# Two-stage MoE after thresholded attention on one core: grouped row blocks, a second place for half of the split weights, a new order

## The chip, the cores and the metric

One NeuronCore of a Trainium2 chip runs the whole program. The metric is device microseconds, from launch to end of one execution; of several executions the median counts.

## The reference, cut to what matters

```python
scores = 1/sqrt(64) * q @ k.T                       # 4 batches x 8 heads, 576 rows, width 64
thresh = max(scores, -1) - tau
scores = where(scores >= thresh, scores, -1e9) - max(...)
attn   = exp(scores); attn = attn / (sum(attn, -1) + 1e-9)
x      = (attn @ v) as 2304 tokens x 512
h = x @ w_in;  g = 0 if h <= -1, h if h >= 1, else (h + 1)**2 / 4;  x = g @ w_out     # first MLP, d_ff 2048
h = x @ w_in2; g = h - tanh(h);                                     out = g @ w_out2  # second MLP
```

The weights come as float64, everything else as float32.

## The kernel before, in words

The matrix products of the MLPs keep float32 accuracy by splitting each operand into a high and a low part (`hi`, `lo`, both float32r) and adding three products: hi x hi, lo x hi, hi x lo.

**MLPs.** The 2304 tokens are five token blocks: the first 512 rows of each of the four batches (blocks 0 to 3) and the four leftovers of 64 rows (block 4, 256 wide). Each MLP has 16 chunks of d_ff, 128 wide, so a block is 2 x 16 = 32 steps, 160 in all; step j has block T, MLP M, chunk s. A step multiplies the block with a chunk of `w_in` into a PSUM bank `ph` (`m_h`), applies the gate (`m_act` on ACT, `m_dve` on DVE), splits the result (`m_split`: copy `gh`, then subtraction `gl`, mostly on POOL) and adds the product with a chunk of `w_out` to four banks `s` (`m_out`).

**Weights.** In block 0 a chunk is loaded raw (`w_load`, two halves into `w64`), decoded from float64 to float32 (`w_dec`: `top` on ACT, then `wr` on DVE) and split (`w_split`: `wi`/`wo`, copy on ACT, subtraction mostly on POOL) into two pairs of hi and lo, one for `w_in` (`wi`), one for `w_out` (`wo`), each 512 KB in a ring of three. `w_store` writes both pairs to DRAM (`wf0i`, `wf0o`, `wf1i`, `wf1o`); blocks 1 to 4 read them back (`w_get`).

**Attention.** The unit is a row block: 128 rows of one head against its 576 keys. `u_qk` on PE writes scores `s`; `u_max` on DVE takes the negated row maximum; `u_exp` on ACT; `u_mask` on DVE applies the threshold, sums the row and turns the sum into a factor `rs` (tensor_scalar, reciprocal, each on one column). Then `u_hi` (ACT) and `u_lo` (POOL) split the weights into two f16 parts `a`, and `u_tr` transposes them by DMA into `at`. Batches 0 and 1 are "narrow" (`NARROW`): per row block, `u_dot` runs 14 products of width 64 into a bank `ph`, and `u_put` on DVE scales the 64 columns into `xw`. Of batch 0's four head pairs the last is `direct`: PE transposes, and there is no f16 split. `v_load`, `v_max`, `v_sc1`, `v_sc2`, `v_split` load and split the values. Batches 2 and 3 are "wide" (`pv`). Batch 0's attention runs ahead of step 0 (below: the prologue), batch 1's beside block 0, batch 2's beside block 1, batch 3's beside block 2, and batch 0's leftover rows beside block 3.

**What sets the order.** `kernel` gives every call a place on a scale of steps (`when`, `at`, L953 on), less a number from the table `PRE` by function and stage. `Program.issue` (L261) then plays the engines forward with assumed durations and lets each take the ready instruction with the lowest number. What comes out is a fixed order for each engine: PE, DVE (VectorE), ACT (ScalarE), POOL (GpSimd) and SP, which issues all DMAs. On the chip each works its order from front to back. The PSUM banks are two `ph` and six in three tiles `s`; `ph` serves gates, products with values and small transposes in turn.

The lines that the steps below touch: `u_mask` L603, `u_tr` L642, `u_dot` L658, `u_put` L677, `v_load` L696, `w_get` L826, `w_dec` L832, `w_store` L846, `w_split` L852. Almost every instruction is recorded by `rec` and so shows as L354 in the profile.

Of the kernel before, what the change touches and what calls it, by code (L numbers as in the profile page):

```python
# [21 lines left out]
D = 64  # L22
# [66 lines left out]
    "load_k": (7.27, -15.44, 8.94, 0.00),  # L89
    "load_q": (3.73, 6.44, 24.95, 0.00),  # L90
    "m_act": (0.00, -5.32, -0.24, -7.95),
    "m_dve": (0.00, 11.52, -21.89, -14.88),
    "m_evac": (0.00, -4.26, 4.07, -23.40),
    "m_h": (0.00, -1.15, -0.74, 2.14),
    "m_out": (0.00, -3.74, -0.36, 2.07),
    "m_split": (0.00, -1.26, 7.97, 1.61),
    "prep_k": (-15.59, 0.87, 7.96, 0.00),
    "prep_q": (21.35, 4.08, -22.11, 0.00),
    "pv": (0.00, 0.00, 2.86, 0.00),
    "u_dot": (-4.92, -3.40, 0.00, 0.00),  # L100
    "u_exp": (23.08, 16.66, 42.89, 0.00),
    "u_hi": (10.52, 34.89, 8.23, 0.00),
    "u_lo": (-15.45, 16.69, 11.25, 0.00),
    "u_mask": (1.51, -2.24, 3.82, 0.00),
    "u_max": (10.16, -1.25, -4.45, 0.00),
    "u_put": (19.81, -1.30, 0.00, 0.00),
    "u_qk": (-1.85, 25.10, 3.18, 0.00),
    "u_tr": (5.19, -3.00, 19.56, 0.00),
    "v_load": (1.71, -6.79, 1.05, 0.00),
    "v_max": (5.82, -0.49, -4.93, 0.00),  # L110
    "v_sc1": (-2.99, 15.36, 1.20, 0.00),
    "v_sc2": (-2.52, -2.20, 18.08, 0.00),
# [16 lines left out]
W_LO = "PVPPPPPVPPVPPPPP"  # L129
UNIT = (0.0, 0.05, 0.1, 0.2, 0.3, 0.4, 0.5)  # L130
# [32 lines left out]
class Program:  # L163
# [169 lines left out]
def attention_moe_moe2(ctx: ExitStack, tc: tile.TileContext, qd, kd, vd, tau, w1, w2, ident, out):  # L333
# [61 lines left out]
    def dve(name, **kw):  # L395
# [26 lines left out]
    def dma(out, in_):  # L422
# [17 lines left out]
    wf = [[dram.tile([NF, 128, 1024], F32, name=f"wf{m}{p}") for p in "io"] for m in range(2)]  # L440
    wr = const("wr", [128, 3, 1024])
# [29 lines left out]
    )  # L471
    m4_r = ring("m4", 2, [4, 1])
# [7 lines left out]
    for b, mains, tail in plan:  # L480
        for hp in range(H // 2):
# [85 lines left out]
    def transpose(out, in_):  # L567
        rec("SP", 1290, nc.sync.dma_start_transpose, serve=1100 * in_.shape[0] * width(in_) / (128 * 1152), out=out, in_=in_)
# [89 lines left out]
    def u_dot(i):  # L658
# [4 lines left out]
        if t.direct:  # L663
            for c in range(5):
                n = 128 if c < 4 else 64
                mm(u.p[:, 0:D], u.et[0:n, 128 * c:128 * c + 128], v.raw[0:n, 2 * (t.hp % 2) + e, c], c == 0, c == 4)
            return
        for x in range(2) if e is None else (e,):
            h = 2 * (t.hp % 2) + x
            o = u.p[:, 64 * x:64 * x + 64] if e is None else u.p[:, 0:64]  # L670
            for c in range(5):
                mm(o, u.at[:, c], v.t[:, h, c, x, :], c == 0, False)
                mm(o, u.at[:, c], v.t[:, h, c, 1 - x, :], False, False)
            for c in range(4):
                mm(o, u.at[:, 5 + c], v.t[:, h, c, x, :], False, c == 3)

    def u_put(i):  # L677
        t, e, m = units[i]
        u = U.pop(i)
        if e is None:  # L680
            t.xt = xt_r()
        elif t.xf is None:
            t.xf = xf_r()
        for x in range(2) if e is None else (e,):
            o = t.xt[:, 64 * x:64 * x + 64] if e is None else t.xf[:, 128 * m + D * e:128 * m + D * e + D]
            src = u.p[:, 64 * x:64 * x + 64] if e is None else u.p[:, 0:64]
            if t.direct:
# [417 lines left out]
```

## Time and profile before

| what | us |
|---|---|
| three runs | 1081.36, 1089.78, 1090.70 |
| median | 1089.78 |
| profiled execution, span from first to last instruction | 1082.6 |
| profiled execution, time of its own | not listed beside its span |
| TensorE busy | 1030.0 |
| ScalarE, VectorE, GpSimd busy | 632.4, 629.2, 504.0 |

How to read it: busy times of different engines overlap, so they don't add up to the span. The engine with the largest share is the one to ask first, but what a change is worth in a stage is decided by the wait that ends last in that stage. The profile counts from the first instruction of the program.

### The profile page before, as it was taken

Reading aid. Unit: us, or ns where it says so; the run is one execution under the profiler, and the core shown is the slowest. Engines: PE = TensorE matmul, PEld = TensorE weight load, DVE = VectorE, ACT = ScalarE, POOL = GpSimd, SP = SyncE. Lnnn points to the kernel's source line nnn. Section 1 sums busy time; section 2 is a strip of 40 time slices with the busy share of each in tenths; the row PEclk is TensorE's granted clock in tenths of the full one; section 3 lists DMA queues with packets and bytes.
Section 4 is the critical chain, followed back from the end, with each engine's and each line's share of the span. In section 5 each row is a group of like instructions: output and inputs, shape, how many; then the busy total and the mean of one; then the engine's idle time right before and its main releaser. Section 6 shows DMA issues by size and latency. Waiting matters only on the chain.

```text
span 1082.6 us, 17257 instructions
## 1 busy us (share of the span) xinstructions
PE 1030.0 (95%) x5826; PEld 831.0 (77%) x5826; DVE 629.2 (58%) x1380; ACT 632.4 (58%) x1158; POOL 504.0 (47%) x510
## 2 busy tenths in 40 slices
PE   5789999999999999999999999999999999998997
PEld 3567777767777788778888888778877878888986
DVE  5987978898898766674347665742253331113432
ACT  5778777768776777676457777764353332222332
POOL 3654778768686555445345555444333212220000
PEclk8999999999999999999999999999999999999999
DMA  6999999999999998889679988897586655557997
GB/s 148 176 229 335 313 319 320 297 275 353 352 336 314 315 243 231 226 227 232 209 206 277 266 212 217 211 230 207 171 269 194 178 189 183 188 193 285 369 343 248
DMA packets 231384, 272.93 MB, mean 252 GB/s; under 512 B 170240, under 2 KB 170368, under 8 KB 231296
## 3 DMA queue, kind: packets, MB, share of 16 engines
q1 hardware_dynamic: 231296, 271.83, 86.5%
q8 instruction: 46, 0.75, 0.3%
q14 instruction: 42, 0.34, 0.1%
HBM read 193.40 MB, written 38.27 MB: 214 GB/s over the span
## 4 chain that ended last, share of the span: by engine, by line
PE 70%; DVE 12%; ACT 8%; DMA 5%; issue 4%; POOL 1%; SPq 0%; ACTq 0%; DVEq 0%; POOLq 0%
PE ph L354 35%; PE s L354 35%; DVE small L354 3%; DMA w<-in_w_dram 2%; ACT e L354 2%; DVE wr L354 2%; DVE e L354 2%; DMA vr<-in_vd_dram 2%; DVE g L354 1%; DVE xw L354 1%; ACT a L354 1%; DVE ph L354 1%; DMA wo<-wf0o 1%; ACT top L354 1%; DMA at<-w 1%
## 5 line engine op out<-in xcount | busy, mean ns | idle before, releaser
L354 PE MATMUL ph<-xh,wi 128*128 128x512 f32 x1024 | 271.1, 399 | 4.0 <-DVE g L354 3.7
L354 POOL TENSOR_TENSOR a<-e,a 128x512 f16<-128x512 f32 x236 | 180.9, 785 | 188.9 <-ACT a L354 172.4
L354 POOL TENSOR_TENSOR gl<-g,gh 128x512 fp32r<-128x512 f32 x114 | 152.3, 1336 | 199.1 <-ACT gh L354 179.4
L354 PEld LDWEIGHTS ph<-xh,wi 128*128 128x128 f32 x1024 | 188.0, 189 | 45.4 <-DVE g L354 6.2
L354 PE MATMUL s<-gh,wo 128*128 128x512 f32 (+1 forms) x640 | 157.4, 377 | 5.2 <-ACT gh L354 1.9
L354 PE MATMUL s<-wo,gh 128*128 128x512 f32 x576 | 155.1, 398 | 1.1 <-ACT w L354 0.7
L354 PE MATMUL ph<-xl,wi 128*128 128x512 f32 x512 | 144.8, 396 | 0.2 <-DVE xl L354 0.2
L354 DVE SCALAR_TENSOR_TENSOR e<-s,small,e 128x576 f32<-128x576 f32 x129 | 104.8, 813 | 67.1 <-ACT small L354 66.4
L354 DVE TENSOR_REDUCE small<-s 128x1 f32<-128x576 f32 x144 | 108.2, 752 | 47.7 <-PE s L354 46.8
L354 ACT ACTIVATE gh<-g 128x512 fp32r<-128x512 f32 (+1 forms) x152 | 88.2, 581 | 78.5 <-DVE g L354 76.2
L354 DVE TENSOR_TENSOR g<-ph,t 128x512 f32<-128x512 f32 (+1 forms) x80 | 50.8, 635 | 142.2 <-ACT t L354 138.9
L354 PEld LDWEIGHTS s<-gh,wo 128*128 128x128 f32 x640 | 112.0, 191 | 26.4 <-ACT gh L354 4.2
L354 PEld LDWEIGHTS s<-wo,gh 128*128 128x128 f32 x576 | 105.2, 188 | 22.9 <-ACT gh L354 1.1
L354 ACT ACTIVATE e<-s,small 128x576 f32<-128x576 f32 x129 | 94.9, 736 | 44.6 <-DVE small L354 41.7
L354 ACT ACTIVATE t<-ph 128x512 f32<-128x512 f32 (+1 forms) x80 | 44.1, 552 | 120.6 <-PE ph L354 120.4
L354 PEld LDWEIGHTS ph<-xl,wi 128*128 128x128 f32 x512 | 95.9, 188 | 23.2 <-DVE xl L354 1.2
L354 PE MATMUL s<-gl,wo 128*128 128x512 f32 (+1 forms) x320 | 89.4, 381 | 4.5 <-ACT xh L354 2.1
L354 DVE TENSOR_TENSOR ph<-ph,t 128x512 f32<-128x512 f32 (+1 forms) x80 | 51.4, 643 | 70.1 <-ACT t L354 69.2
L354 ACT ACTIVATE t<-ph,small 128x512 f32<-128x512 f32 (+1 forms) x80 | 51.4, 642 | 66.4 <-PE ph L354 66.2
L354 ACT ACTIVATE a<-e 128x576 f16<-128x576 f32 x118 | 80.1, 679 | 6.8 <-DVE e L354 4.8
L354 PE MATMUL s<-wo,gl 128*128 128x512 f32 x288 | 82.3, 393 | 1.0 <-ACT w L354 1.0
L354 PEld LDWEIGHTS s<-gl,wo 128*128 128x128 f32 x320 | 57.6, 190 | 15.8 <-ACT xh L354 3.4
(107 smaller groups left out, 1513.6 us busy)
## 6 DMA issues: line engine op xcount, KB each, us to landing
w<-in_w_dram SPq DMA_DIRECT2D x64, 512.0 KB, 6.0
wi<-wf0i SPq DMA_DIRECT2D x64, 512.0 KB, 4.1
wo<-wf0o SPq DMA_DIRECT2D x64, 512.0 KB, 4.3
wi<-wf1i SPq DMA_DIRECT2D x64, 512.0 KB, 3.8
wo<-wf1o SPq DMA_DIRECT2D x64, 512.0 KB, 3.7
kr<-in_kd_dram SPq DMA_DIRECT2D x32, 288.0 KB, 4.4
wf0i<-wi SPq DMA_DIRECT2D x16, 512.0 KB, 6.1
wf0o<-wo SPq DMA_DIRECT2D x16, 512.0 KB, 5.6
```

What stands on the lines that cost most here:

```text
L354: P.add(eng, dur, lambda: fn(**kw), outs, ins, serve, lock, load)
```

## The change: what it does

**Grouping.** In narrow attention the four row blocks of one head form a group. `u_mask` only sums into one column of a [128, 4] tile. `g_rs` makes one tensor_scalar and one reciprocal on four columns, `g_dot` runs all four blocks' products into four 64-wide parts of one bank, `g_put` scales 256 columns in one tensor_tensor with a broadcast factor. The leftover row blocks keep `u_dot` and `u_put`.

**Odd chunks.** Of the chunks with odd s, block 0 stores the decoded float32 (`wr` to `wg0`, `wg1`, 512 KB) and not the two pairs. Block 1 loads that, splits it again (`w_late`: two copies on ACT, one subtraction on POOL, one on DVE) and stores the pairs, which blocks 2 to 4 read as before.

**Order.** `PRE` has a column for every 16 steps in place of four stages, with new numbers, and the assumed durations differ.

```diff
-    "u_exp": (23.08, 16.66, 42.89, 0.00),
+    "u_exp": (162.91, 1.78, 106.82, 40.43, 29.55, 75.76, 86.55, 77.7, 44.6, 0, 0),
...
+LATE = (1,)
+W_LO_LATE = "PV"
+LATE_AT = (2.6, 1.4)
...
-            begin = max(self.dma, t + (1000 if turn else 900))
+            begin = max(self.dma, t + (1050 if turn else 1250))
...
     def u_mask(i):
+        t, e, m = units[i]
         u = U[i]
-        u.sum = sum_r()
-        u.rs = rs_r()
+        grouped = e is not None and not t.wide
+        if grouped:
+            if m == 0:
+                t.groups[e].sum = gs_r()
+            u.sum = t.groups[e].sum[:, m:m + 1]
+        else:
+            u.sum = sum_r()
+            u.rs = rs_r()
         dve("scalar_tensor_tensor", out=u.e, in0=u.s, scalar=u.thr, in1=u.e, op0=ALU.is_ge, op1=ALU.mult, accum_out=u.sum
         )
+        if grouped:
+            return
...
+    def g_rs(g):
+        t = g.t
+        g.rs = gr_r()
+        h = 2 * (t.hp % 2) + g.e
+        scale = 1.0 if t.direct else VQ[t.ph, t.hp // 2].sc[:, h:h + 1]
+        dve("tensor_scalar", out=g.sum, in0=g.sum, scalar1=1e-9, scalar2=scale, op0=ALU.add, op1=ALU.mult)
+        dve("reciprocal", out=g.rs, in_=g.sum)
+
+    def g_dot(g):
...
+        g.p = ph_r()
+        for m in range(4):
+            u = U.pop(g.first + m)
+            o = g.p[:, 64 * m:64 * m + 64]
+            if t.direct:
+                for c in range(5):
+                    n = 128 if c < 4 else 64
+                    mm(o, u.et[0:n, 128 * c:128 * c + 128], v.raw[0:n, h, c], c == 0, c == 4)
+            else:
+                dot(o, u.at, v, h, e)
+
+    def g_put(g):
...
+        dve("tensor_tensor", out=t.xf.rearrange("p (m c) -> p m c", m=4)[:, :, D * e:D * e + D],
+            in0=g.p[:, 0:256].rearrange("p (m c) -> p m c", m=4),
+            in1=g.rs.rearrange("p (m o) -> p m o", o=1).to_broadcast([128, 4, D]), op=ALU.mult)
...
+        if T == 1 and late(s):
+            w.f = wr_r()
+            dma(w.f, wg[M][s])
...
-        dma(w_pair(W[j], p), wf[M][p][s])
+        if T > 1 or not late(s):
+            dma(w_pair(W[j], p), wf[M][p][s])
...
             T, M, s = steps[j]
+            if late(s):
+                dma(wg[M][s], W[j].f)
+                return
             for p in range(2):
                 dma(wf[M][p][s], W[j].flat[p])
...
+    def w_late(j, p):
+        T, M, s = steps[j]
+        w = W[j]
+        w.flat[p] = w_pair(w, p)
+        f = w.f[:, 512 * p:512 * p + 512]
+        act(out=w.hi[p], in_=f, func=AF.Copy)
+        sub(pick(W_LO_LATE, p), w.lo[p], f, w.hi[p].bitcast(F32))
+        dma(wf[M][p][s], w.flat[p])
...
-        stage = 0 if k < 0 else 1 if k < 32 else 2 if k < 128 else 3
-        P.at = k - PRE.get(fn.__name__, (0, 0, 0, 0))[stage]
+        stage = 0 if k < 0 else min(1 + int(k) // NF, 10)
+        P.at = k - PRE[fn.__name__][stage]
```

Over the whole program PE's instructions are the same in number and kind. DVE loses 64 reciprocals and 64 tensor_scalars on one column and 64 products of width 64, and gains 16 each on four columns, 16 products of width 256 and 16 subtractions for `wo`. ACT gains 32 copies, POOL 16 subtractions for `wi`. SP has 630 DMAs before and after; 32 loads of pairs become 16 loads from `wg` and 16 stores to it.

VectorE in the prologue, where the first head's row blocks are finished (`s` scores, `e` and `wr` exponentials, `small` row statistics, `xw` the attention output, `v` split values). Before:

```order
L354 TENSOR_SCALAR xw<-ph_138,small 128x64
L354 TENSOR_SCALAR small<-small 128x1 x2
L354 RECIPROCAL small<-small 128x1
L354 TENSOR_SCALAR kr_112<-kr_112,small 128x576
L354 TENSOR_SCALAR xw<-ph_139,small 128x64
L354 TENSOR_REDUCE small<-s_140 128x1
L354 TENSOR_SCALAR xw<-ph_138,small 128x64
L354 RECIPROCAL small<-small 128x1 x2
L354 SCALAR_TENSOR_TENSOR e_123,small<-s_142,small,e_123 128x576
L354 TENSOR_SCALAR xw<-ph_139,small 128x64
```

VectorE at the same place after the change:

```order
L361 SCALAR_TENSOR_TENSOR e_127,small<-s_143,small,e_127 128x576
L361 TENSOR_SCALAR small<-small 128x4 x2
L361 TENSOR_REDUCE small<-s_142 128x1
L361 RECIPROCAL small<-small 128x4 x2
L361 SCALAR_TENSOR_TENSOR v_135<-vr_134,small,v_135 128x5x64 x2
L361 TENSOR_REDUCE small<-s_143 128x1
L361 SCALAR_TENSOR_TENSOR v_135<-vr_134,small,v_135 128x5x64 x2
L361 TENSOR_TENSOR xw<-ph_140,small 128x4x64
```

Four products of one head have become one, and two heads' tensor_scalars and reciprocals on four columns stand together.

SP's queue in the prologue, from the fourth transpose of the first head (`at` from `w` or `a`) to the fourth of the second; `kr`, `t`, `g`, `qr` are keys and queries, `vr` values. Before:

```order
L354 DMA_TRANSPOSE at_129<-w_97 128x9x128
L354 DMA kr_112<-in_kd_dram 64x576 x2
L354 DMA t_105<-in_qd_dram 64x512
L354 DMA_TRANSPOSE at_130<-w_97 128x9x128
L354 DMA vr_132<-in_vd_dram 128x1280
L354 DMA_TRANSPOSE at_130<-w_97 128x9x128
L354 DMA g_106<-in_qd_dram 64x512
L354 DMA qr_120<-in_qd_dram 128x2x576
L354 DMA_TRANSPOSE at_130<-w_97 128x9x128 x2
```

SP at the same place after the change:

```order
L361 DMA_TRANSPOSE at_131<-w_99 128x9x128
L361 DMA kr_114<-in_kd_dram 64x576
L361 DMA_TRANSPOSE at_132<-w_99 128x9x128 x4
L361 DMA_TRANSPOSE at_133<-w_99 128x9x128
L361 DMA_TRANSPOSE at_133<-a_128 128x9x128
```

The four transposes follow each other; the loads that stood among them have moved behind. At the very start the first load of `vr`, eighth in the queue before, is sixth now.

SP's queue early in block 1 (`wi`, `wo` pairs, `wf0i`, `wf0o` their place in DRAM). Before:

```order
L354 DMA wo_101<-wf0o 128x1024
L354 DMA vr_132<-in_vd_dram 128x1280
L354 DMA wi_100<-wf0i 128x1024
L354 DMA kr_112<-in_kd_dram 128x576
L354 DMA wo_102<-wf0o 128x1024
L354 DMA_TRANSPOSE at_130<-a_127 128x9x128
L354 DMA wi_98<-wf0i 128x1024
```

SP at the like place after the change:

```order
L361 DMA wo_104<-wf0o 128x1024
L361 DMA_TRANSPOSE at_131<-a_128 128x9x128
L361 DMA wr<-wg_96 128x1024
L361 DMA wf0o<-wo_103 128x1024
L361 DMA kr_115<-in_kd_dram 128x576
L361 DMA wi_102<-wf0i 128x1024
L361 DMA wr<-wg_96 128x1024
```

Where a pair was loaded for each chunk, every second chunk now has one load of float32 (`wr<-wg`) and two stores of pairs (`wf0o<-wo`, `wf0i<-wi`) in the same queue.

## Rows read from the trace of the kernel before

**Rows 1.** Page, part 1: busy time of each engine, share, instructions.

```profile
PE 1030.0 (95%) x5826; PEld 831.0 (77%) x5826; DVE 629.2 (58%) x1380; ACT 632.4 (58%) x1158; POOL 504.0 (47%) x510
```

**Rows 2.** Windows: stretch, length, busy PE, PEld, DVE, ACT, POOL; clock; DMA share; GB/s.

```profile
0.00:100.30 100.30, 76.94 (x612) 57.03 (x613) 78.86 (x231) 69.04 (x136) 51.67 (x71) 0.91 0.89 207
100.30:339.10 238.80, 226.58 (x1492) 178.44 (x1491) 202.33 (x405) 178.24 (x321) 182.01 (x158) 0.98 1.07 326
339.10:568.70 229.60, 226.24 (x1110) 182.37 (x1109) 135.51 (x295) 154.28 (x274) 113.83 (x125) 1.00 0.89 238
568.70:788.90 220.20, 217.83 (x1066) 175.32 (x1065) 120.72 (x266) 140.58 (x250) 108.10 (x116) 1.00 0.83 224
788.90:977.00 188.10, 186.49 (x877) 149.38 (x875) 54.65 (x101) 60.24 (x107) 48.41 (x43) 1.00 0.64 198
977.00:1082.60 105.60, 95.87 (x678) 88.41 (x677) 37.11 (x86) 30.04 (x71) 0.00 (x0) 1.00 0.86 313
```

**Rows 3.** Windows, the prologue from 16 us on in two stretches.

```profile
16.00:72.00 56.00, 42.99 (x404) 29.35 (x403) 51.98 (x166) 43.48 (x85) 38.78 (x51) 0.93 0.97 186
72.00:100.30 28.30, 27.16 (x195) 23.09 (x194) 21.15 (x53) 21.32 (x45) 9.46 (x8) 0.89 0.89 279
```

**Rows 4.** Timeline of DVE, 0 to 72 us: start, length, instruction, [idle before].

```profile
12.08 1.49 DVE L354 TENSOR_REDUCE small<-vr 128x4 f32<-128x1280 f32 x1 [3.65 <-DMA vr<-in_vd_dram]
...
18.02 0.15 DVE L354 RECIPROCAL small<-small 128x1 f32<-128x1 f32 x1
18.09 0.13 DVE L354 TENSOR_SCALAR small<-small 128x1 f32<-128x1 f32 x1
18.14 0.81 DVE L354 SCALAR_TENSOR_TENSOR e<-s,small,e 128x576 f32<-128x576 f32 x1
...
38.79 0.34 DVE L354 TENSOR_SCALAR xw<-ph,small 128x64 f32<-128x64 f32 x1 [2.39 <-PE ph L354]
39.05 0.15 DVE L354 RECIPROCAL small<-small 128x1 f32<-128x1 f32 x1
```

**Rows 5.** Groups by shape, DVE: count, busy us, mean ns, idle before; whole span.

```profile
L354 DVE TENSOR_TENSOR ph<-ph,t 128x256 f32<-128x256 f32 x16 | 6.9, 432 | 19.0 <-ACT t L354 19.0
```

**Rows 6.** Timeline of SP's queue, 0 to 44 us: start, length of issue, DMA.

```profile
3.73 0.60 SPq L354 DMA_DIRECT2D kr<-in_kd_dram  x1
4.37 0.59 SPq L354 DMA_DIRECT2D idt<-in_ident_dram  x1
5.00 0.43 SPq L354 DMA_DIRECT2D vr<-in_vd_dram  x1
...
30.02 0.36 SPq L354 DMA_DIRECT2D vr<-in_vd_dram  x1
30.49 1.30 SPq L354 DMA_TRANSPOSE at<-w  x1
```

**Rows 7.** Timeline of PE, a product with values that waited for a transpose.

```profile
37.82 0.93 PE L354 MATMUL ph<-v,at 128*128 128x64 f16 x14 [2.83 <-DMA at<-w]
```

**Rows 8.** Waits from 100.3 to 339.1 us: us in total, times, longest.

```profile
PE ph L354 <- DVE g L354: 3.8, 3, 2.0
PE s L354 <- DVE e L354: 2.9, 4, 2.0
...
ACT top L354 <- DMA w<-in_w_dram: 13.7, 10, 3.0
```

**Rows 9.** Page, part 6: DMA issues, count, KB each, median us to landing.

```profile
w<-in_w_dram SPq DMA_DIRECT2D x64, 512.0 KB, 6.0
wi<-wf0i SPq DMA_DIRECT2D x64, 512.0 KB, 4.1
...
wo<-wf1o SPq DMA_DIRECT2D x64, 512.0 KB, 3.7
...
vr<-in_vd_dram SPq DMA_DIRECT2D x10, 640.0 KB, 5.1
```

**Rows 10.** Groups by shape: splitting a decoded chunk on ACT, POOL and DVE.

```profile
L354 ACT ACTIVATE wi<-wr 128x512 fp32r<-128x512 f32 x32 | 20.0, 625 | 5.7 <-DVE wr L354 5.2 <-POOL gl L354 0.4
...
L354 POOL TENSOR_TENSOR wi<-wr,wi 128x512 fp32r<-128x512 f32 x28 | 38.9, 1393 | 16.7 <-ACT wi L354 16.7
...
L354 DVE TENSOR_TENSOR wo<-wr,wo 128x512 fp32r<-128x512 f32 x8 | 7.1, 889 | 0.0
```

More of the change, by code (lines that the diff above doesn't have):

```diff
@@ L88 @@
 PRE = {
[L89 to L100, printed above, removed]
@@ L101 @@
-    "u_exp": (23.08, 16.66, 42.89, 0.00),
[L102 to L112, printed above, removed]
@@ new lines @@
+    "w_dec": (0.55, -2.04, -27.13, 0, 0, 0, 0, 0, 0, 0, 0),
+    "w_get": (0, 111.48, 19.23, 115.94, 59.3, 20.55, 4.64, 97.59, 37.97, 73.59, 43.97),
+    "w_late": (0, 0, 30.69, 3.91, 61.36, 0, 0, 0, 0, 0, 0),
+    "w_load": (-7.02, 86.35, -16.38, 36.54, -3.25, 0, 0, 0, 0, 0, 0),
+    "w_split": (-2.24, -1.82, -4.07, 0, 0, 0, 0, 0, 0, 0, 0),
+    "w_store": (-48.34, -7.08, 32.65, 0, 0, 0, 0, 0, 0, 0, 0),
+    "x_split": (78.07, 72.36, 147.5, 38.37, -48.74, 1.97, -52.49, 29.23, -29.81, 0, 0),
+    "x_tail": (0, 52.4, 34.99, 0, 0, 0, 0, 0, 0, 0, 0),
@@ L403, in dve @@
             dur = n / (1.92 if fast else 0.96) + 150 + 50 * ("accum_out" in kw)
-            dur += 60 * (fast and any(isinstance(kw.get(k), AP) for k in ("scalar1", "scalar2")))
+            scalars = sum(isinstance(kw.get(k), AP) for k in ("scalar", "scalar1", "scalar2"))
+            dur += 60 * (scalars > 0 and "accum_out" not in kw) + 55 * (scalars > 1)
         rec("DVE", dur, getattr(nc.vector, name), lock=n > 8 and on_chip and (fast or len(ins) == 2), **kw)
@@ L425, in dma @@
             n *= d
-        rec("SP", 590 if n < 200e3 else 345, nc.sync.dma_start, serve=max(n / 415.0, 130) + 150 * (n < 400e3), out=out, in_=in_)
+        rec("SP", 683 if n < 200e3 else 438, nc.sync.dma_start, serve=max(n / 345.0, 130) + 150 * (n < 400e3), out=out, in_=in_)
     idt = const("idt", [128, 128])
-    small = const("small", [128, 64])
+    small = const("small", [128, 80])
     tau_t, taun, tneg, qsc, half, none = (small[:, i:i + 1] for i in range(6))
@@ L440, in attention_moe_moe2 @@
     wf = [[dram.tile([NF, 128, 1024], F32, name=f"wf{m}{p}") for p in "io"] for m in range(2)]
+    wg = [dram.tile([NF, 128, 1024], F32, name=f"wg{m}") for m in range(2)]
     wr = const("wr", [128, 3, 1024])
@@ L471, in attention_moe_moe2 @@
     )
+    gs_r = Ring(lambda i: small[:, 52 + 4 * i:56 + 4 * i], 3)
+    gr_r = Ring(lambda i: small[:, 64 + 4 * i:68 + 4 * i], 3)
     m4_r = ring("m4", 2, [4, 1])
@@ L493, in attention_moe_moe2 @@
             t.done = [len(units) - 1] * 2
+            t.groups = []
             for e in range(2 if mains else 0):
+                if not t.wide:
+                    t.groups.append(Obj())
+                    t.groups[e].t, t.groups[e].e, t.groups[e].first = t, e, len(units)
                 for m in range(4):
@@ L567, in transpose @@
     def transpose(out, in_):
-        rec("SP", 1290, nc.sync.dma_start_transpose, serve=1100 * in_.shape[0] * width(in_) / (128 * 1152), out=out, in_=in_)
+        rec("SP", 1290, nc.sync.dma_start_transpose, serve=1200 * in_.shape[0] * width(in_) / (128 * 1152), out=out, in_=in_)
     def u_qk(i):
@@ L662, in u_dot, with dot @@
         u.p = ph_r()
[L663 to L668, printed above, removed]
-            h = 2 * (t.hp % 2) + x
[L670 to L675, printed above, removed]
+        for x in range(2):
+            h = 2 * (t.hp % 2) + x
+            o = u.p[:, 64 * x:64 * x + 64]
+            dot(o, u.at, v, h, x)
+    def dot(o, at, v, h, x):
+        for c in range(5):
+            mm(o, at[:, c], v.t[:, h, c, x, :], c == 0, False)
+            mm(o, at[:, c], v.t[:, h, c, 1 - x, :], False, False)
+        for c in range(4):
+            mm(o, at[:, 5 + c], v.t[:, h, c, x, :], False, c == 3)
     def u_put(i):
@@ L819, in w_load, with late @@
             dma(w.f, (w1, w2)[M][s])
+    def late(s):
+        return s % 2 in LATE
     def w_pair(w, p):
@@ L975, in attention_moe_moe2 @@
             at(k + o, fn, i)
-        if not units[i][0].wide:
-            k = snap(k + lag(units[i][0]))
-            at(k, u_dot, i)
-            at(k, u_put, i)
+        t, e, m = units[i]
+        if not t.wide:
+            k = snap(k + lag(t))
+            if e is None:
+                at(k, u_dot, i)
+                at(k, u_put, i)
+            elif m == 3:
+                at(k, g_rs, t.groups[e])
+                at(k, g_dot, t.groups[e])
+                at(k, g_put, t.groups[e])
     for t in touches:
@@ L1024, in attention_moe_moe2 @@
         for p in range(2):
-            at(max(j - GET[p], 2 * NF - 1 - spl + 0.05), w_get, j, p)
+            first = 2 * NF - 1 - spl + 0.05
+            at(max(j - GET[p], first), w_get, j, p)
+            if T == 1 and late(s):
+                at(max(j - LATE_AT[p], first), w_late, j, p)
     P.at = -1e3
```

61 lines of the change are left out of this document (40 added, 21 removed).

## The prediction

> **What bounds the kernel now.** I read the busy times of the page first, then the busy times by stage, then inside the first two stages the waits, the timeline and the DMA queue.
>
> TensorE (PE) is busy for 1030.0 us of a span of 1082.6 [rows 1]. Its work is not touched, so only the 52.6 us in which it sits idle, and what a lower granted clock stretches, can be won. The stage view [rows 2] cuts the span at the first gate matmul of each token block. Its columns show where that idle time lies: 23.4 us in the prologue (100.3 - 76.9), 12.2 in token block 0 (238.8 - 226.6), 3.4, 2.4 and 1.6 in blocks 1 to 3, 9.7 in block 4. The granted clock averages 0.91 in the prologue and 0.98 in block 0; it has two levels, 2.4 and 1.2 GHz, so part of both stages ran at the lower. From block 1 on it is 1.00. So four fifths of what can be won lies ahead of 339 us.
>
> In the prologue the middle stretch decides [rows 3]: from 16 to 72 us VectorE (DVE) is busy 51.98 of 56 us and PE 42.99. There DVE sets the pace. From 72 to 100 it is PE (27.16 of 28.3), and a faster DVE buys nothing. In block 0 PE is at 95%, DVE at 85% (202.33 of 238.8), and the DMA share is 1.07, against 0.64 to 0.89 in blocks 1 to 3: packets overlap there, the queues are full.
>
> **The change part by part.** The profile names no time for the profiled execution beside its span, 1082.6. The lowest run is 1.2 us below that, the median of the runs 7.2 above. I sum against the span and add 3, the middle of these two distances.
>
> *Prologue, grouping.* For each of the 64 main row blocks in narrow attention DVE now runs a small tensor_scalar, a reciprocal and a 64-wide product. Rows 4 give what each holds of the engine, start to start: reciprocal 0.07 (18.02 to 18.09), tensor_scalar 0.05 (to 18.14), product 0.26 (38.79 to 39.05); 0.38 in all. After the change four row blocks share one set. The pair on four columns I take at the same 0.12. The 256-wide product is not in the trace; the nearest row, a 256-wide tensor_tensor out of PSUM, takes 0.432 us [rows 5], and with the 0.08 by which the 64-wide product's next neighbour starts before its end (0.34 - 0.26) that is 0.35. Bounds: 0.26 and 4 x 0.26. So 0.47 a group. Batch 0 has 32 blocks in 8 groups: 32 x 0.38 - 8 x 0.47 = 8.4 us less for DVE. Three of its four head pairs lie in the stretch where DVE sets the pace: 6.3.
>
> The Trainium skill's page "VectorE: DVE Perf Modes" (The DRAIN you can't avoid) says that after every op the pipe must empty before the next starts, and that op count is what to cut. By it the whole lengths count, 0.60 a block and 0.71 a group, and batch 0 would save 32 x 0.60 - 8 x 0.71 = 13.5 us, not 8.4. Rows 4 speak against it: an op of 0.15 us is followed by the next start after 0.07. The page itself adds that an op that is not held starts earlier.
>
> What hides the 6.3? The DMA share of the same stretch is 0.97 [rows 3]. At block 0's full level of 1.07 that work needs 56 x 0.97 / 1.07 = 50.8 us, which would stop the gain at 5.2; but weights for later lie in it too. I keep 6.3. The price of grouping is a wait: the products of four blocks stand behind the last of four transposes, and scores of later blocks stand behind them on PE. In the new order of SP four transposes of the second head follow the first four with one small load between, where before six loads stood ahead of and among them, one of 640 KB issued at 30.02 [rows 6, 9]; PE waited 2.83 us for one of them [rows 7]. I call wait and gain even (bounds -2.8 and +4).
>
> *Prologue, start.* The first value load moves ahead of a k half and the identity. Before it was issued at 5.00, two issues later than now (3.73) [rows 6], and DVE sat 3.65 us until it landed [rows 4]: -1.3. Prologue: -7.6, bounds -13 (all of PE's idle time from 16 to 72) and +2.
>
> *Block 0.* Batch 1 has as many groups, so DVE loses another 8.4 us. The 16 odd chunks store 0.5 MB and not 1: 8.4 MB less. At the stage's own 326 GB/s [rows 2] that is 25.8 us of DMA. PE's waits in this stage end mostly with DVE (3.8 for the gate, 2.9 for a mask), and behind them ACT waited 13.7 us for raw weights [rows 8], whose loads take 6.0 us to land against 3.7 for a half pair read back later [rows 9]. The removed stores stand on the very queue that these loads pass. To win are 12.2 us of idle and some 4.8 of clock (238.8 x 0.02). PE stays the bound, so I take half: -8, bounds -14 and +5 (a worse order).
>
> The Trainium skill's page "DMA: Bandwidth & Descriptors" (Bandwidth) puts a core's limit on HBM at about 358 GB/s. By it the stage's 77.8 MB need 217 us of 238.8, DMA is not what is late, and only DVE's part is won: block 0 about -4, the whole sum -9.6. The share of 1.07 speaks against it; no run here shows the stage with fewer stores.
>
> *Block 1.* Its odd chunks come as 0.5 MB, are split again and stored as pairs. ACT gets 32 copies of 0.625 (20.0 us), POOL 16 subtractions of 1.393 (22.3), DVE 16 of 0.889 (14.2) [rows 10]. Beside the stage's busy times [rows 2] that makes ACT 174 of 229.6 us, POOL 136, DVE 150: room on each, PE at 98.5% hides them. DMA gains 8.4 MB, 25.8 us; 0.89 x 229.6 + 25.8 is a share of 1.00. Waits added: a copy on ACT for its pair slot, behind which stand exponentials and gates; a store on SP for its POOL subtraction, behind which stand transposes and the even chunks' loads. Nearest row: block 0, which had both and idled 5.1% against 1.5%. So the bounds are 0 and +8.3, and since DVE is far from block 0's 85% I take +3.
>
> *Blocks 2 to 4.* Only order. 4 us of idle in 408 for blocks 2 and 3, 9.7 in block 4, part of it evacuations that nothing covers: -1, bounds -4 and +4.
>
> Sum: -7.6 - 8 + 3 - 1 = -13.6; span 1069.0, time 1072.0.
>
> **Rivals.** *Hidden anyway.* In the prologue transposes, not DVE, are the limit (DMA share 0.97 speaks for it, DVE's 52 of 56 against), and block 0 stays bound by PE: -3 - 2 + 3 + 0 = -2, time 1083.6.
>
> *Nearly all goes.* DVE and DMA stood behind nearly every PE wait of the first two stages, and with them the clock stays up: -13 - 14 + 0 - 1 = -28, time 1057.6. Rows 8 speak for it, the wait lists name DVE in most cases; against it that PE at 95% rarely comes to 100% with three other engines near it.
>
> *The late split is late.* In block 1 each odd chunk's pair passes ACT, then POOL, in queues that run in order, in a slot that comes free only when the third chunk before is used up. If each of 16 makes PE wait x, the stage costs 16x in place of 3: -16.6 + 16x. From x = 1.04 the span is longer than before; at the 2.2 us that 0.625 + 1.393 and a hand-over come to, it is +18.6, time 1104.2, slower. For it: ACT at 76% in order. Against: the load that it replaces took 4.1 us into the same slot [rows 9], more than the split.
>
> **How the numbers follow.** Forecast 0.52, nearly all 0.17, hidden 0.18, late split 0.13. About 1% (1078.9 to 1100.7) is what a measurement of this kernel tells from no change. The forecast's own spread, about 7 us, leaves 0.44 of its 0.52 below 1078.9; with 0.17 and 0.02 from "hidden" that is 0.64 faster (rounded up by 0.01). Same: 0.08 + 0.15 + 0.03 = 0.26. Slower: 0.10, all from the late split. Range: down to 1053 for "nearly all", up to 1090, which leaves out most of the late split. The forecast alone: 1063 to 1081.
>
> **What would show it.** Right: the first gate matmul at 92 to 94 us, not 100.3; DVE's busy time in the prologue down by 6 to 9; block 0 in about 231 us at a DMA share near 1.0, with fewer ACT waits for raw weights; block 1 at 231 to 234 with a share near 1.0. Wrong: a first gate matmul after 98 with PE waiting for transposes (grouping only moved the wait); block 0 no shorter though DMA has room (PE or order bound); block 1 over 240 with PE waiting for a pair that ACT or POOL wrote.

## The result, and the profile after

The changed kernel takes 1073.16 us (median of four runs, 1071.43 to 1075.31), the kernel before 1088.31 in the same comparison: a ratio of 0.9873, 95% interval 0.9838 to 0.9908. So it is 1.3% faster, and the forecast of 1072.0 holds. The profiled execution of before was a short one for that kernel (span 1082.6 where the median run takes 1088.3), that of after a long one (span 1073.5, time 1075.31). The two traces therefore show 9.1 us of difference, the medians 15.2.

TensorE's granted clock, averaged over a whole execution, goes with this: in 60 executions of the kernel before whose clock is on record (one of 3529 us is left out) it is 0.980 to 0.993, with a median time of 1092 us at 0.982 (seven executions) and 1082.5 at 0.990 (three). The changed kernel's ten, those of after_again below included, have 0.990 to 0.996; the two at 0.990 took 1072.7 and 1075.8. So at a like clock the kernels lie some 8 us apart by these few, and the rest of the 15 comes together with less time at 1.2 GHz. Which of the two brings the other no run separates.

The page's busy times of the changed kernel, to set beside [rows 1]:

```profile
PE 1025.9 (96%) x5826; PEld 826.2 (77%) x5826; DVE 633.2 (59%) x1252; ACT 646.2 (60%) x1190; POOL 531.1 (49%) x526
```

Its stages, cut like [rows 2] at the first gate matmul of each token block (prologue, blocks 0, 1, 2, then 3 and 4), and the middle of the prologue, which answers to [rows 3]:

```profile
core 0: us, PE busy (x) PEld busy (x) DVE busy (x) ACT busy (x) POOL busy (x), PEclk, DMA share, GB/s
0.00:94.00 94.00, 73.11 (x615) 55.45 (x615) 71.86 (x158) 68.72 (x139) 50.97 (x70) 0.95 0.95 213
94.00:330.00 236.00, 225.30 (x1500) 180.27 (x1499) 201.76 (x335) 178.39 (x321) 186.48 (x158) 0.99 1.04 301
330.00:559.80 229.80, 224.93 (x1100) 180.14 (x1099) 147.11 (x309) 168.99 (x303) 138.54 (x142) 1.00 0.95 268
559.80:781.70 221.90, 220.39 (x1076) 175.17 (x1075) 124.24 (x275) 145.56 (x263) 112.00 (x119) 1.00 0.88 227
781.70:1073.50 291.80, 282.14 (x1543) 235.21 (x1541) 88.21 (x177) 84.54 (x168) 43.08 (x38) 1.00 0.71 239
16.00:66.00 50.00, 37.22 (x330) 26.13 (x328) 45.22 (x104) 40.09 (x80) 35.40 (x48) 0.92 1.13 199
```

Against [rows 2], the prologue is 6.3 us shorter, block 0 2.7 us; block 1 is 0.2 us longer, block 2 1.7 us longer, the rest 1.9 shorter. DVE's busy time fell by 7.0 us in the prologue but by only 0.6 in block 0. Block 0 moves 301 GB/s at a share of 1.04 where it moved 326 at 1.07. Its waits, beside [rows 8]:

```profile
engine line waited for: us in total, times, longest us
...
ACT top L361 <- DMA w<-in_w_dram: 8.1, 5, 3.7
...
PE s L361 <- DVE e L361: 4.1, 7, 1.6
```

ScalarE's wait for raw weights is down from 13.7 us to 8.1; TensorE waits longest for VectorE's masks (4.1, before 2.9). So the trace confirms the direction of the two large steps, and leaves open what made the gain: fewer operations on VectorE, fewer bytes, or the order.

### The profile page after: what moved, and what is told of

Read it like the earlier page. It is cut to its first block, busy times and chain, and to the rows that moved or that the text cites. A ratio compares the mean times of both kernels' runs of the same rounds, so it can differ in the third digit from the quotient of the medians.

```text
span 1073.5 us, 17195 instructions
## 1 busy us (share of the span) xinstructions
PE 1025.9 (96%) x5826; PEld 826.2 (77%) x5826; DVE 633.2 (59%) x1252; ACT 646.2 (60%) x1190; POOL 531.1 (49%) x526
## 4 chain that ended last, share of the span: by engine, by line
PE 74%; DVE 11%; ACT 5%; issue 4%; DMA 3%; POOL 2%; SPq 1%; DVEq 0%; ACTq 0%; POOLq 0%
PE s L361 38%; PE ph L361 36%; DVE small L361 3%; DVE e L361 2%; DVE wr L361 1%; ACT e L361 1%; DMA w<-in_w_dram 1%; DMA vr<-in_vd_dram 1%; DVE g L361 1%; POOL a L361 1%; DVE ph L361 1%; ACT t L361 1%; SPq L361 1%; ACT xh L361 1%; POOL gl L361 0%
## 5 line engine op out<-in xcount | busy, mean ns | idle before, releaser
L361 PE MATMUL ph<-xh,wi 128*128 128x512 f32 x1024 | 274.3, 400 | 1.5 <-ACT wi L361 1.1
L361 POOL TENSOR_TENSOR a<-e,a 128x512 f16<-128x512 f32 x236 | 186.0, 810 | 117.8 <-ACT a L361 100.5
L361 PE MATMUL ph<-xl,wi 128*128 128x512 f32 x512 | 148.5, 398 | 2.5 <-DVE xl L361 2.4
L361 ACT ACTIVATE e<-s,small 128x576 f32<-128x576 f32 x129 | 94.7, 734 | 32.3 <-DVE small L361 30.6
L361 PE MATMUL s<-gl,wo 128*128 128x512 f32 (+1 forms) x320 | 85.4, 373 | 1.8 <-ACT xh L361 1.4
L361 ACT ACTIVATE e<-e,small 128x576 f32<-128x576 f32 x76 | 58.8, 773 | 34.5 <-DVE small L361 34.3
```

The costliest lines, as they stand in the source:

```text
L361: P.add(eng, dur, lambda: fn(**kw), outs, ins, serve, lock, load)
```

## The experiments

Each kernel's ratio is to executions of the kernel before on the same chip. In the table, a stage runs from one first gate matmul to the next in one profiled execution, the last column holds blocks 3 and 4.

| kernel | median | ratio (95%) | prologue | block 0 | block 1 | block 2 | rest |
|---|---|---|---|---|---|---|---|
| before | 1086.9 to 1088.4 | 1 | 100.3 | 238.8 | 229.6 | 220.2 | 293.7 |
| after | 1073.16 | 0.9873 (0.9838-0.9908) | 94.0 | 236.1 | 229.8 | 221.9 | 291.8 |
| after_again | 1072.9 | 0.9871 (0.9837-0.9904) | 90.1 | 236.1 | 229.8 | 221.8 | 293.3 |
| e_cols | 1074.75 | 0.9877 (0.9837-0.9917) | 90.8 | 239.7 | 229.8 | 221.3 | 293.5 |
| e_singles | 1075.87 | 0.9896 (0.9862-0.9930) | 93.6 | 235.4 | 229.8 | 221.9 | 293.0 |
| e_store2 | 1083.94 | 0.9955 (0.9929-0.9980) | 92.5 | 241.0 | 229.7 | 222.4 | 294.6 |
| less_bytes | 1079.87 | 0.9932 (0.9901-0.9963) | 99.3 | 234.6 | 228.6 | 220.8 | 297.3 |
| group_alone | 1084.10 | 0.9956 (0.9935-0.9977) | 95.1 | 243.2 | 230.6 | 220.2 | 295.7 |
| late_alone | 1095.18 | 1.0068 (1.0048-1.0087) | 97.8 | 246.5 | 233.4 | 220.5 | 294.1 |
| old_order | 1089.80 | 1.0029 (1.0005-1.0053) | 92.8 | 246.9 | 229.6 | 220.0 | 296.1 |
| no_late | 1103.02 | 1.0157 (1.0127-1.0187) | 93.2 | 260.4 | 236.1 | 221.5 | 293.1 |
| no_group | 1106.53 | 1.0186 (1.0150-1.0222) | 94.7 | 262.3 | 233.4 | 222.3 | 293.0 |
| late_twice | 1093.37 | 1.0063 (1.0037-1.0089) | 93.5 | 233.4 | 248.7 | 221.9 | 292.1 |
| late_none | 1071.75 | 0.9844 (0.9813-0.9875) | 92.3 | 236.7 | 227.5 | 222.2 | 292.6 |

Two readings come before any verdict. A stage of a single execution is good to a few us: the five kernels with the changed kernel's order and bytes in block 0 (after, after_again, e_cols, late_twice, late_none) have it at 233.4 to 239.7, and the prologue of one and the same kernel is 94.0 or 90.1. Block 1 is steadier: 229.7 or 229.8 in the five that keep its order and work (after, after_again, e_cols, e_singles, e_store2). And totals are compared by medians and ratios, not by spans.

**after_again.** The changed kernel, unaltered.

> The changed kernel once more, unaltered, as the mark for the other kernels of this call. Every theory expects the same: a ratio to the kernel before of 0.985 to 0.990 (the first four runs gave 0.9873), so 1071 to 1076 us where the kernel before takes 1088; first gate matmul at 93 to 95 us, block 0 at 235 to 238 us, and 4-column tensor_scalars of about 0.58 us mean, up to 1.2 us.

The time repeated. The prologue did not, and the view by stretches shows why:

```profile
0.00:90.10 90.10, 70.00 (x614) 53.25 (x615) 71.21 (x158) 68.61 (x138) 51.06 (x71) 0.98 0.97 223
90.10:326.30 236.20, 225.43 (x1502) 180.27 (x1501) 201.73 (x335) 178.48 (x321) 186.48 (x158) 0.99 1.04 300
```

Nearly the same matmuls (614 and 615 on record) took 70.0 us at a mean granted clock of 0.98, not 73.1 at 0.95. Part of this stage runs at 1.2 GHz in one execution and less of it in the next.

**e_cols and e_singles: VectorE's work, in the changed kernel's order.** The first splits only the 4-column tensor_scalar; the second restores all of VectorE's single operations.

```diff
 # both
-dve("tensor_scalar", out=g.sum, in0=g.sum, scalar1=1e-9, scalar2=scale, ...)
+for m in range(4): nc.vector.tensor_scalar(out=out[:, m:m+1], in0=in0[:, m:m+1], ...)
 # e_singles only
-dve("reciprocal", out=g.rs, in_=g.sum)
+for m in range(4): nc.vector.reciprocal(out=out[:, m:m+1], in_=in_[:, m:m+1])
-dve("tensor_tensor", out=t.xf..., in0=g.p..., in1=g.rs..., op=ALU.mult)
+for m in range(4): nc.vector.tensor_scalar(out=out[:, m], in0=in0[:, m], scalar1=in1[:, m:m+1], ...)
```

> The 4-column tensor_scalar of each group is issued as four of one column each; every engine's order stays. In the changed kernel the 16 of them took 0.578 us mean, and each long one ended 20 to 60 ns after a GpSimd instruction that was running ended, while the one-column form took 0.149 us. Theory 'the 4-column form waits for GpSimd': the four one-column ones take 0.15 us each and overlap, no one above 0.25 us; the 3.1 us gap of TensorE at 59.7 us in the prologue falls under 2 us; the sum is 2 to 5 us shorter than the changed kernel. Rival 'VectorE was only held up by its input, the width does not matter': the long ones stay long as the first of four, and the time stays within 1 us.

The groups by line of after (busy us, mean ns of one, idle before), then that of e_cols, whose loop is line 718:

```profile
L361 DVE TENSOR_SCALAR small<-small 128x4 f32<-128x4 f32 x16 | 9.1, 578 | 0.0
L361 DVE RECIPROCAL small<-small 128x4 f32<-128x4 f32 x16 | 2.6, 167 | 0.1
```

```profile
L718 DVE TENSOR_SCALAR small<-small 128x1 f32<-128x1 f32 x64 | 8.4, 192 | 0.0
```

The first half of the theory holds: no one-column operation took over 0.21 us, so for this step the width makes the wait. The second half fell: 64 short ones kept VectorE 8.4 us, the 16 long ones 9.1, so nearly nothing was freed, TensorE's gap behind them went from 3.2 us (after_again) to 2.2 and not under 2, and the time stayed (0.9877 against 0.9871).

> The changed kernel's order and row blocks in one bank, but VectorE's work as before the change: per group four one-column tensor_scalars, four one-column reciprocals and four products of 64 columns in place of one of each. Theory 'VectorE sets the prologue and block 0, and the grouping is what it gained': against the changed kernel VectorE's busy time grows by about 0.5 us per group (four products of 0.26 for one of 0.35, less what the 4-column tensor_scalar had lost), so by 4 us in the prologue and 4 us in block 0, and three quarters of it reach the end: 5 to 7 us longer than the changed kernel. Rival 'the gain is the new order and the DMA bytes': no more than 1.5 us longer.

The view of stretches of e_singles, with the windows of after:

```profile
0.00:94.00 94.00, 73.28 (x616) 55.28 (x616) 76.86 (x231) 70.24 (x139) 51.41 (x72) 0.94 0.92 214
94.00:330.00 236.00, 225.93 (x1503) 179.13 (x1502) 208.12 (x407) 178.64 (x322) 185.50 (x159) 0.99 1.07 302
```

Block 0's VectorE busy time rose from 201.8 to 208.1 us, the first 94 us' from 71.9 to 76.9. The median rose by 3.0 us, between the two expectations, and the intervals overlap (0.9862 to 0.9930 against 0.9837 to 0.9904); the profiled execution shows no stage that pays. So VectorE's part of the grouping is worth some 3 us to this order, as near as can be told, though it frees 5 to 6 us of VectorE in either stage.

**e_store2 and less_bytes: the bytes, each in an order kept as it was.** The first gives block 0 of the changed kernel its 8.4 MB back, the second takes 8.4 MB from block 0 of the kernel before.

```diff
 # e_store2
-dma(wg[M][s], W[j].f)
+nc.sync.dma_start(out=wg[M][s], in_=W[j].f); nc.sync.dma_start(out=wx[M][s], in_=W[j].f)
 # less_bytes, on the kernel before, s odd
-for p in range(2): dma(wf[M][p][s], W[j].flat[p])
+dma(wf[M][0][s], W[j].flat[0])
-dma(w_pair(W[j], 1), wf[M][1][s])
+dma(w_pair(W[j], 1), wf[M][0][s])
```

> In block 0 each odd chunk's 512 KB are stored twice, the second time into a buffer that nothing reads (an extra, unused copy), so that block 0 moves as many bytes as the kernel before: 16 x 0.52 = 8.4 MB more, 25.8 us of transfer at the 325 GB/s of the kernel before in that stage. Everything else stands in the changed kernel's order. Theory 'DMA sets block 0': block 0 is 4 to 8 us longer than the changed kernel's 236 us and ScalarE's waits for raw weights rise from 8.1 toward 13.7 us. Rival 'TensorE sets block 0, the bytes are hidden': block 0 within 1 us of the changed kernel's, at a DMA share over 1.08, and the total within 1.5 us.

> The kernel before with one thing less: of each odd chunk only the first of the two 512 KB pairs is stored in block 0, and the later blocks load the first pair a second time where the second would be wanted (so odd chunks use wrong weights from block 1 on; all other work and every engine's order stay as before, and blocks 1 to 4 load as many bytes). 8.4 MB less in block 0, as in the changed kernel. Theory 'DMA sets block 0 in the old order too' (8.4 MB more cost the changed kernel 11 us in the median): 6 to 11 us shorter than the kernel before, block 0 at 229 to 234 us in place of 238.75. Rival 'the old order has its waits elsewhere, and bytes are worth something only to an order that counts on them' (TensorE's waits there were mostly for VectorE's e and g): 0 to 3 us shorter.

Block 0 of e_store2 by the view of stretches:

```profile
92.50:333.50 241.00, 224.53 (x1502) 178.99 (x1501) 201.16 (x335) 178.25 (x321) 181.48 (x158) 0.99 1.07 326
```

One of its waits there:

```profile
ACT top L361 <- DMA w<-in_w_dram: 18.9, 14, 5.0
```

The same of less_bytes, whose helper stands on line 354 as before:

```profile
99.30:333.90 234.60, 224.42 (x1491) 177.17 (x1490) 203.25 (x404) 178.34 (x321) 182.70 (x158) 0.99 1.03 300
```

And its wait:

```profile
ACT top L354 <- DMA w<-in_w_dram: 7.2, 6, 2.5
```

With the bytes, block 0 stands at 326 GB/s and 1.07 in the changed kernel as in [rows 2], ScalarE waits 18.9 us for raw weights, and the median is 11.0 us longer. Without them, the old order shows 300 GB/s, 7.2 us of that wait where [rows 8] have 13.7, and a median 8.5 us shorter (7.4 by the ratio). In the profiled executions block 0 itself is 4.9 us longer and 4.2 shorter, at 234.6 just outside the 229 to 234 expected of less_bytes. VectorE's busy time is hardly touched in either (201.2 and 203.3). So 8.4 MB in block 0 are worth 7 to 11 us in either order, some third of the 25.8 us that they take to move. The Trainium skill's page "DMA: Bandwidth & Descriptors" (Bandwidth) gives about 358 GB/s per core, and says that this holds when both cores of a pair stream. Read as a limit, it would leave DMA room at 326 GB/s and make the bytes worth nothing; these runs don't bear that out, and a stretch of no_late (below) moves 382 GB/s.

**group_alone, late_alone, old_order: the parts in the old order.** The kernel before's table and assumed durations, with the first part, the second, and both.

```diff
 # all three: PRE, stages and assumed durations of the kernel before, with
+"g_dot": (-4.92, -3.40, 0, 0), "g_put": (19.81, -1.30, 0, 0), "g_rs": (19.81, -1.30, 0, 0), "w_late": (0, 0, 0, 0)
 # group_alone
-LATE = (1,)
+LATE = ()
 # late_alone: u_mask, u_dot, u_put of the kernel before, called for every row block
```

> The kernel before with the first part alone: grouping, with the lead times and costs of the kernel before (the group's steps get the lead of those they replace); odd chunks as before. Prediction's own terms: prologue 6.3 shorter, block 0 about 6 shorter, so 1076 us. Theory 'an order that was not fitted to the parts loses what they save' (old order with both parts was 3 us longer than the kernel before, prologue 7.6 shorter, block 0 8 longer): prologue 4 to 8 us shorter, block 0 0 to 8 longer, 1080 to 1092 us.

> The kernel before with the second part alone: late odd chunks, with the lead times and costs of the kernel before; row blocks not grouped. Prediction's own terms: block 0 shorter by what the bytes give (8 or less), block 1 3 longer: 1081 to 1088 us. Theory 'an order that was not fitted to the parts loses what they save': block 0 within 4 us of 238.75 or longer, block 1 0 to 5 us longer, 1086 to 1096 us.

> The changed kernel with the table of lead times and the planner's costs of the kernel before (new steps get the lead of the steps they replace); grouping and late odd chunks stay. Theory 'the order is worth what is left' (15 us in all, 11 by the bytes, 3 by VectorE's work): 0 to 3 us longer than the changed kernel, 1073 to 1076 us, first gate matmul at 95 to 99 us since the first value load stands late again. Rival 'the order is what gained': 8 us or more longer, 1081 and up.

Grouping alone gains 4 us (0.9956); in the profiled execution the prologue gains 5.3 and block 0 loses 4.5. Late odd chunks alone cost 7 us, both together 3. So the two parts together earn nothing under the old table, although each removes the work that it should. The theory of the first two expectations held, and in old_order the rival: it is 17 us longer than the changed kernel. Block 0 of old_order by the view of stretches:

```profile
92.80:339.60 246.80, 228.23 (x1503) 182.43 (x1502) 204.82 (x349) 185.12 (x336) 186.76 (x164) 0.97 1.00 289
```

TensorE's waits there (us in total, times, longest):

```profile
PE s L361 <- DVE e L361: 7.8, 5, 2.4
PE ph L361 <- DVE g L361: 3.6, 3, 1.6
PE s L361 <- DVE gh L361: 2.1, 1, 2.1
```

DMA has room now (1.00), but the stage is 8 us longer than before: TensorE waits 7.8 us for masks where [rows 8] show 2.9, at a clock of 0.97. The lead numbers decide which of several ready instructions an engine takes, and with the new steps in the pool they pick another order, which is worse. ("Old order" is short for the old table: no engine's order here is that of the kernel before.) The new table without either part was not run.

**no_late and no_group: the new order without one part.** They are the changed kernel with `LATE = ()`, and with the row blocks ungrouped as in late_alone.

> The changed kernel without its second part: block 0 splits and stores odd chunks as the kernel before did, block 1 loads pairs; grouping, new order and the planner's new costs stay. Theory 'DMA sets block 0' (the unused second copy cost 11 us in the median, 4.9 of it in block 0): 8 to 13 us longer than the changed kernel, 1081 to 1086 us, block 0 at 240 to 246 us, DMA share there over 1.06. Prediction's own terms (block 0 -8, block 1 +3): 5 us longer, 1078. Rival 'the odd chunks cost as much late as they save early': within 1.5 us of the changed kernel.

> The changed kernel without its first part: each main block has its own reciprocal, scaling and product and leaves its bank by itself, as before the change; late odd chunks, new order and costs stay. Theory 'the grouping gained little' (undoing VectorE's part of it alone cost 3 us in the median): 2 to 5 us longer than the changed kernel, 1075 to 1078 us. Prediction's own term (prologue -6.3, three quarters of VectorE's 8.4 in block 0): 8 to 12 us longer, 1081 to 1085.

Both expectations missed by far: 30 and 34 us longer than the changed kernel, and slower than the kernel before. Most of it is block 0 (24 and 26 us), some of it block 1 (6 and 4). In no_late the loss in block 0 is mostly in one place, seen in two stretches:

```profile
195.00:232.00 37.00, 31.01 (x162) 23.30 (x162) 23.28 (x38) 20.63 (x37) 21.58 (x18) 0.86 1.04 382
232.00:262.00 30.00, 8.83 (x50) 6.53 (x49) 13.14 (x25) 13.86 (x24) 9.69 (x10) 0.55 0.83 259
```

TensorE's waits from 230 to 262 us:

```profile
PE s L361 <- DVE kh L361: 12.2, 1, 12.2
PE s L361 <- DVE e L361: 8.1, 3, 2.7
```

SyncE's timeline ahead of it (start, length of the issue):

```profile
200.68 2.62 SPq L361 DMA_TRANSPOSE at<-a  x1
203.35 0.57 SPq L361 DMA_DIRECT2D wf0i<-wi  x1
203.97 0.42 SPq L361 DMA_DIRECT2D wf0o<-wo  x1
...
208.28 2.26 SPq L361 DMA_DIRECT2D w<-in_w_dram  x2
...
234.91 0.32 SPq L361 DMA_DIRECT2D wf1o<-wo  x1
235.32 1.51 SPq L361 DMA_DIRECT2D w<-in_w_dram  x2
236.88 0.46 SPq L361 DMA_DIRECT2D kr<-in_kd_dram  x1
```

From 203.35 to 236.88 us SyncE issues 26 stores and raw loads and nothing for attention. The k half that the next heads need goes out at 236.88; the one before it had gone at 88.65. (In the changed kernel four go out between, at 142.27, 183.27, 188.86 and 221.34.) TensorE runs out of scores, waits 12.2 us, then three times 2.7 for masks, and its granted clock, 0.86 on the mean in the stretch before, falls to 0.55 in that of the waits: nine tenths of it at 1.2 GHz.

In no_group there is no such hole. Its block 0 by the view of stretches:

```profile
94.70:357.00 262.30, 235.67 (x1490) 184.89 (x1491) 205.40 (x419) 186.72 (x334) 186.96 (x166) 0.93 1.00 283
```

TensorE's three largest waits there:

```profile
PE s L361 <- DVE e L361: 10.2, 10, 3.0
PE s L361 <- ACT gh L361: 4.5, 2, 3.7
PE ph L361 <- DVE xw L361: 3.9, 8, 0.7
```

TensorE idles 26.6 us here, in many short waits, and its clock averages 0.93. Set beside e_singles, this is the plainest case of the study: VectorE runs as many single operations per row block in both, the bytes are the same, and the medians are 1106.5 and 1075.9. What differs is how the row blocks share banks and, with it, the order on every engine. The first of these was not run by itself.

**late_twice and late_none: the price of the late split.** The changed kernel with each copy and subtraction of `w_late` issued twice, and not at all.

```diff
 # late_twice
-act(out=w.hi[p], in_=f, func=AF.Copy); sub(pick(W_LO_LATE, p), w.lo[p], f, w.hi[p].bitcast(F32))
+the same two instructions, each issued twice in a row
 # late_none
-act(out=w.hi[p], in_=f, func=AF.Copy); sub(pick(W_LO_LATE, p), w.lo[p], f, w.hi[p].bitcast(F32))
```

> Every step of the late split in block 1 is done twice (ScalarE's copy and the subtraction on GpSimd or VectorE repeated with the same operands and result): 32 copies of 0.625, 16 subtractions of 1.393 on GpSimd and 16 of 0.889 on VectorE more in block 1; the order stays. Own theory (TensorE sets block 1, busy 224.9 of 229.8 us there): block 1 0 to 1.5 us longer, total within 2 us of the changed kernel. Rival 'the late split is late' with x us per odd chunk: block 1 longer by 16 x its extra 0.6 to 2.0 us, so 10 to 32 us.

> The changed kernel with the late split left out of block 1: ScalarE's 32 copies and the 32 subtractions are not issued (the pairs are stored and used with what the buffers held); loads, stores and every engine's order stay. Own theory 'TensorE sets block 1, a single late split is hidden' : block 1 within 1.5 us of the changed kernel's 229.8, total within 2 us. Rival 'the late split already costs' (done twice it cost 19 us in block 1): block 1 3 to 5 us shorter, which is all that TensorE idles there (4.9 us).

Block 1 of late_twice by the view of stretches:

```profile
326.90:575.60 248.70, 229.12 (x1099) 180.34 (x1098) 162.01 (x325) 187.46 (x335) 160.52 (x158) 1.00 0.90 248
```

TensorE's two largest waits there:

```profile
PE ph L361 <- DVE g L361: 6.7, 7, 2.1
PE s L361 <- DVE e L361: 6.0, 8, 1.5
```

Block 1 of late_none:

```profile
329.00:556.50 227.50, 223.89 (x1099) 180.34 (x1098) 132.02 (x293) 153.68 (x272) 114.59 (x126) 1.00 0.97 271
```

The first split costs block 1 2.3 us (227.5 to 229.8, clear of the 0.1 by which this stage varies), a second 18.9. My own expectation for late_twice fell, and late_none came out between its two. Even doubled, no engine is full (ACT 187 of 249), and TensorE waits most not for the split pair but for VectorE's gates and masks. That these stand behind the extra work in VectorE's and ScalarE's queues is argued from the order, not measured by itself.

## Why the prediction was right, and where it was not

**The total** was forecast at -13.6 us and is -15.2 by the medians. The range and the side were right. By stages the sum fits less well than its total, and that the total came so near is in part luck: the pair of traces, from which the stages below are taken, shows 9.1 us and not 15.2. With the order held, taking a part back costs 11.0 us by the medians (the bytes) and 3.0 (VectorE's single operations) and gives 1.2 (the late split), some 13 of the 15. One reading of the rows was off: of the 52.6 us of TensorE's idle time 35.6 lie ahead of 339 us, two thirds and not four fifths (three quarters with 9.0 and 4.8 us for the clock).

**Prologue, -7.6.** Right in size: the first gate matmul stands at 94.0 and 90.1 us in two executions and between these in e_cols, e_store2, late_twice and late_none, forecast 92 to 94, and VectorE's busy time fell by 7.0, forecast 6 to 9. The 8.4 us for VectorE was near, though one term in it was not: "The pair on four columns I take at the same 0.12." The tensor_scalar alone took 0.578 us mean. The 256-wide product took 0.42, as the row said. The start, -1.3, was right in size too. VectorE's first maximum of the values begins, in after,

```profile
9.02 1.49 DVE L361 TENSOR_REDUCE small<-vr 128x4 f32<-128x1280 f32 x1 [0.55 <-DMA vr<-in_vd_dram]
```

and not at 12.08 [rows 4]; but the load lands at very different times, and over all runs the start lies at 10.05 to 12.08 us in the five with the old table and at 8.41 to 10.62 in the nine with the new one, 1.6 earlier on the mean.

But the cause was read too narrowly. The sum put 6.3 of the 7.6 down to grouping. The old order with grouping gets to 95.1 us (92.8 with both parts), the new order without it to 94.7, and with VectorE's single operations back to 93.6. Either of the two buys 5 to 6 us, more than half of the gain; they don't add. In the new order 5 us more of VectorE's work did not show in the prologue. Its middle stretch now has a DMA share of 1.13 against the 0.97 of [rows 3], over the 1.07 that the prediction took for the full level when it weighed this limit and set it aside. Whether DMA now sets this stretch was not tested.

**Block 0, -8.** This is the step that failed: 2.7 us in the pair of traces, where the stage was to take 231; none of the five kernels that share the changed kernel's block 0 (named under the table) gets under 233.4. (Some of the 4 us by which the profiled execution of before undercuts its median may lie here; no run shows it, and with all of them it would be 6.6.) Two of its terms were sound when measured alone: the bytes are worth 7 to 11 us in an unchanged order, VectorE's work some 3. VectorE's busy time, though, was to fall by 8.4 and fell by 0.6, while against e_singles, in the same order, it is 6.3 lower. The groups of block 0 show two things in the way, first in before, then in after:

```profile
L354 DVE TENSOR_TENSOR wo<-wr,wo 128x512 fp32r<-128x512 f32 x7 | 6.4, 919 | 0.0
```

```profile
L361 DVE TENSOR_TENSOR wo<-wr,wo 128x512 fp32r<-128x512 f32 x7 | 8.6, 1233 | 0.1
L361 DVE TENSOR_SCALAR small<-small 128x4 f32<-128x4 f32 x8 | 4.8, 596 | 0.0
```

The eight tensor_scalars on four columns take 4.8 us, where their pairs with the reciprocals were put at 1.0 in all. And steps that the change leaves as they are take longer, the `wo` subtractions most in sum; why was not tested. What the step lacked besides was a term for the order. It appears in it only as the bound "+5 (a worse order)". By the runs, the same two parts in the old order come to 1.0029 and in the new one to 0.9871, 17 us apart, 11 of them in block 0 by the traces.

**Block 1, +3.** Found +0.2. The term itself was nearly right: the late split costs 2.3 us. The stage without it is 2.1 us shorter than before (227.5), which the prediction had not foreseen.

**Blocks 2 to 4, -1.** Found -0.2 (1.7 longer, then 1.9 shorter).

**The rivals.** "Hidden anyway" fell: 1083.6 is far outside the interval, though its -2 for block 0 is nearer to the traces than the forecast's -8. "Nearly all goes" did too. "The late split is late" names a real mechanism: at twice the work, block 1 pays 1.3 us per odd chunk (21.2 over 16), more than the 1.04 from which it decides. At the work that the change has, x is 0.14 us (2.3 over 16). The busy shares alone did not tell the two cases apart. Yet the rival put the wait at the split pair, and the doubled run shows it at the gate and the masks.

## What to carry to other kernels

Where a planner writes out the order, a change to the work and the table that it was tuned with are one thing: here the parts alone came to -4, +7 and +3 us, the table without one of them to +16 and +20, and all of it to -15. To price a part, hold every engine's order fixed and add or take away only that work, as e_store2, less_bytes and late_none do; removing it from the source measures the planner's next order as well. And busy shares don't say how much more an engine takes: 2.3 us for the first late split, 18.9 for the second, with no engine but TensorE over 76% busy.

## What the runs showed of the hardware that was not expected

A tensor_scalar on 128 x 4 in SBUF takes 0.17 to 0.22 us where GpSimd is idle and up to 1.26 us where it is not. First VectorE's timeline in after_again (start and length in us, xcount), where two groups' tensor_scalars run back to back:

```profile
57.01 2.09 DVE L361 TENSOR_SCALAR small<-small 128x4 f32<-128x4 f32 x2
```

GpSimd's timeline in after_again at the same time:

```profile
56.57 1.40 POOL L361 TENSOR_TENSOR kl<-kr,kh 128x576 fp32r<-128x576 f32 x1
57.93 1.41 POOL L361 TENSOR_TENSOR w<-wr,w 128x512 f16<-128x512 f32 x2
```

VectorE's timeline in e_cols, for the same two groups:

```profile
58.73 1.05 DVE L718 TENSOR_SCALAR small<-small 128x1 f32<-128x1 f32 x8
```

In after_again the first of the two begins while the `kl` subtraction runs and ends 23 ns after it; the second begins there and ends 25 ns after the first `w` subtraction. Of the 16 in this execution nine took over 0.225 us, and each of the nine ended 22 to 32 ns after a GpSimd instruction did. Eight of one column pass in 1.05 us at the same place. And four columns pass too where the source is in PSUM (`ph`): in e_cols, VectorE's timeline

```profile
57.80 0.12 DVE L361 TENSOR_SCALAR small<-ph 128x4 f32<-128x4 f32 x1
```

lies within GpSimd's

```profile
56.78 1.42 POOL L361 TENSOR_TENSOR w<-wr,w 128x512 f16<-128x512 f32 x2 [1.37 <-ACT w L361]
```

None of the ten of this kind in that execution took over 0.14 us, and no reciprocal on 128 x 4 in SBUF took over 0.18. The Trainium skill's page "SBUF — State Buffer" (Who interferes with whom) says that a tensor_scalar in a mode that uses two ports and a GpSimd instruction lock each other out for a whole instruction, and its page "VectorE: DVE Perf Modes" (What auto-detection actually checks) that the mode is taken when a single source and the destination are in SBUF, with outermost sizes that are even or equal. Four columns in SBUF fit that, a source in PSUM does not, and the trace agrees. Whether the rule takes in one column is not plain from the page; here it did not wait. The step on four columns was not tried with its source in PSUM.
